# A fused attention and mixture-of-experts kernel: the order of the squares, of the values' norm and of the scales while the weights are prepared

## The chip, the core and the metric

The kernel runs on one core of one Trainium2 chip. The metric is the device time of one execution in microseconds (us), as the median of several runs. Before the change three runs gave 891.67 us in the median, from 890.34 to 894.32.

## What is computed

```python
# attention per batch and head: B=4, H=8, S=576, D=64, M=32
a      = softmax(phi, axis=s)                 # over the 576 positions
k_m    = a^T k ;  v_m = a^T v                 # 32 memory rows each
attn   = softmax(q k_m^T / sqrt(D))           # over the 32 rows
x      = attn v_m                             # (2304, 512) over batches and heads
# gated layer
x      = (sigmoid(x @ w_gate) * (x @ w_val)) @ w_out     # d_ff = 1536
# routed layer, 8 experts, two per token
logits = x @ w_gate + log1p(exp(x @ w_noise)) * noise
top 2 of 8, their softmax as weights
out   += weight * (relu(x @ w1[e]) @ w2[e])              # F = 1024
```

The inputs of the gated layer arrive as 64-bit words, which the kernel reads as pairs of 32-bit words, a low and a high one.

## The kernel before, in words

The program is written in Python generators that are advanced in turns. A scheduler then gives each engine a fixed queue: TensorE (PE), VectorE (DVE), ScalarE (ACT), GpSimd (POOL), and SyncE (SP), which issues nearly all transfers. An engine takes its queue strictly in order, so an instruction that waits holds up all behind it.

The part that the change touches is the first one, the preparation of the gated layer's weights beside the attention of batches 0 and 1.

- **Loads.** 18 blocks of weights (gate and value of six units `u`, then the six blocks of w_out) come as 36 halves of 512 KB through a ring of four buffers (`ws2`, `WB = 4`). `wload_next` asks for one more half after each half is rounded. A load waits until POOL is done with the buffer that it writes to.
- **Rounding** (`rounded`, L325 to L333). Of each half, ACT turns the low words into numbers (L329), DVE puts the high words together in two instructions (L331, L332), and POOL adds both (L333).
- **Norms.** After both halves of a block, ACT squares it with a sum (`AF.Square`, L363 for gate and value, L359 for w_out). `norm2` adds these sums over the partitions by a small matmul (`pmx`, L87), and three or four tiny DVE instructions (L92 to L96) make of that a power of two and its inverse. `values_scale` (L223) does the same with the values' memory rows of a batch, which gives `sv0` for batch 0. `finish` does it for one unit, `w0` to `w5`.
- **Fold** (`fold`, L231). For batch b and unit u, PE multiplies the weights by the values' rows (`pv`, L243). A scale `ws`, made by DVE from unit and batch (L236), goes into `split`: ACT writes the high half-precision part of the product (`wq`, L376), DVE the low part (L377). That is done in four pieces. The tiles `ws` come from a ring of four.
- **Stage 1** (`stage1`, L410). For each third of a batch (a chunk of 192 columns), 24 matmuls (L424) fill two accumulators, ACT takes the tanh with the scale `gs` (L427, made by `gate_scale` at L388 on first use), DVE multiplies (L429), and ACT and DVE write the two parts of `gT` (L430, L431).
- **Stage 2** (`stage2`, L442) multiplies `gT` by the prepared w_out. For that all of w_out has to be rounded, normed and split (`wo`, L376 and L377).

`build` sets the turns. While batch 0's attention runs, and then beside each chunk of batch 0, the generator `weights` is advanced a few steps; each `yield` in it is one step. It has three steps a block here, and three more for each unit's norm. The routed layer follows at about the middle of the span.

## Time and profile before

| | |
|---|---|
| median of the runs | 891.67 us |
| profiled execution | 891.72 us |
| its span, first to last instruction | 889.9 us |
| PE, DVE, ACT, POOL busy | 814.8, 473.5, 456.8, 208.6 us |
| matmuls, DVE, ACT, POOL instructions | 6531, 1317, 907, 210 |
| PE busy, tenths in the first seven slices of 22 us | 5 5 5 8 8 5 9 |

A share of busy time is one of the whole span. In the first 150 us PE is busy for half to nine tenths, and after that almost always, so a stretch's own rows tell more than the sums.

### The profile page before, as it was taken

Reading aid. Unit: us, or ns where it says so; the run is one execution under the profiler, and the core shown is the slowest. Engines: PE = TensorE matmul, PEld = TensorE weight load, DVE = VectorE, ACT = ScalarE, POOL = GpSimd, SP = SyncE. Lnnn points to the kernel's source line nnn. Section 1 sums busy time; section 2 is a strip of 40 time slices with the busy share of each in tenths; the row PEclk is TensorE's granted clock in tenths of the full one; section 3 lists DMA queues with packets and bytes.
Section 4 is the critical chain, followed back from the end, with each engine's and each line's share of the span. In section 5 each row is a group of like instructions: output and inputs, shape, how many; then the busy total and the mean of one; then the engine's idle time right before and its main releaser. Section 6 shows DMA issues by size and latency. Waiting matters only on the chain. (4 is left out here: it accounts for less than half of the span.)

```text
span 889.9 us, 16827 instructions
## 1 busy us (share of the span) xinstructions
PE 814.8 (92%) x6531; PEld 534.0 (60%) x6531; DVE 473.5 (53%) x1317; ACT 456.8 (51%) x907; POOL 208.6 (23%) x210
## 2 busy tenths in 40 slices
PE   5558859999999998898998999999999999999995
PEld 4347746757657765666655656665747556574752
DVE  1788788555647686874443138553444345340110
ACT  3477667615545476672323348564646446461320
POOL 1363440001110201023014443202323122332112
PEclk9998778999999999999999999999999999999998
DMA  9478639324221564546594869826565868473113
GB/s 317 151 258 292 227 115 341 132 75 102 25 78 25 166 214 142 168 166 194 145 346 107 176 132 263 200 95 143 129 188 120 166 141 214 71 117 48 25 13 47
DMA packets 126067, 135.16 MB, mean 152 GB/s; under 512 B 71968, under 2 KB 88480, under 8 KB 125472
## 3 DMA queue, kind: packets, MB, share of 16 engines
q1 hardware_dynamic: 116000, 113.30, 43.9%
q0 software_dynamic: 9984, 20.75, 12.9%
q8 instruction: 52, 0.85, 0.4%
q14 instruction: 31, 0.25, 0.1%
HBM read 87.97 MB, written 30.86 MB: 134 GB/s over the span
## 5 line engine op out<-in xcount | busy, mean ns | idle before, releaser
L424 PE MATMUL pg<-x,wq 128*128 128x192 f16 x1728 | 174.0, 258 | 23.4 <-ACT wq L376 15.1
L424 PEld LDWEIGHTS <-wq 128*128 128x128 f16 x1728 | 152.5, 103 | 44.2 <-ACT wq L376 17.7
L778 PEld LDWEIGHTS <-hT 128*128 128x128 f16 (+1 forms) x960 | 99.8, 105 | 104.8 <-DVE hT L770 0.9
L442 PE MATMUL px<-wo,gT 128*128 128x512 f16 x648 | 148.8, 379 | 0.3 <-issue 0.3
L784 POOL DMA_INDIRECT out<-y,mts x40 | 64.6, 1614 | 208.7 <-ACT y L783 206.9
L778 PE MATMUL py<-w2a,hT 128*128 128x512 f16 (+1 forms) x480 | 105.2, 379 | 0.4 <-DVE hT L770 0.4
L778 PE MATMUL py<-w2b,hT 128*128 128x512 f16 (+1 forms) x480 | 104.9, 379 | 0.0
L764 PE MATMUL ph<-xe,w1a 128*128 128x312 f16 (+2 forms) x768 | 103.3, 296 | 0.0
L770 DVE TENSOR_TENSOR hT<-r,hT 128x312 f16<-128x312 f32 (+2 forms) x128 | 57.4, 480 | 85.9 <-ACT hT L769 84.5
L764 PE MATMUL ph<-xe,w1b 128*128 128x312 f16 (+2 forms) x768 | 103.0, 296 | 0.0
L442 PEld LDWEIGHTS <-gT 128*128 128x128 f16 x648 | 61.5, 98 | 68.6 <-issue 4.5
L783 ACT ACTIVATE y<-py,css 128x512 f32<-128x512 f32 (+1 forms) x40 | 27.5, 687 | 129.6 <-PE py L778 120.6
L764 PEld LDWEIGHTS <-w1b 128*128 128x128 f16 x768 | 75.2, 98 | 27.1
L764 PEld LDWEIGHTS <-w1a 128*128 128x128 f16 x768 | 75.0, 98 | 27.1
L768 ACT ACTIVATE r<-ph 128x312 f32<-128x312 f32 (+2 forms) x128 | 49.7, 428 | 76.5 <-PE ph L764 73.0
L586 POOL DMA_INDIRECT meta<-mt,vi x36 | 36.1, 1003 | 173.8 <-DVE vi L583 46.4
L749 POOL DMA_INDIRECT xg<-xs,mts x40 | 44.4, 1110 | 87.7 <-DMA xe<-xg 49.0
L427 ACT ACTIVATE sg<-pg,gs 128x384 f32<-128x384 f32 x72 | 41.6, 578 | 41.9 <-PE pg L424 27.9
L429 DVE SCALAR_TENSOR_TENSOR pg<-sg,pg 128x384 f32<-128x384 f32 x72 | 40.2, 558 | 36.8 <-PE pg L424 25.7
L781 DVE TENSOR_TENSOR css<-mts,iw 128x1 f32<-128x1 f32 (+1 forms) x40 | 6.5, 164 | 89.5 <-ACT y L783 84.9
L430 ACT ACTIVATE gT<-pg 128x384 f16<-128x384 f32 x72 | 34.8, 485 | 36.7 <-DVE pg L429 34.4
L769 ACT CAST hT<-r 128x312 f16<-128x312 f32 (+2 forms) x128 | 53.1, 458 | 0.8
(311 smaller groups left out, 972.9 us busy)
## 6 DMA issues: line engine op xcount, KB each, us to landing
wo<-w SPq DMA_DIRECT2D x48, 512.0 KB, 5.5
st<-kv SPq DMA_DIRECT2D x16, 512.0 KB, 7.8
f<-w SPq DMA_DIRECT2D x16, 512.0 KB, 3.8
wsp<-hl SPq DMA_DIRECT2D x16, 512.0 KB, 3.5
w<-wg SPq DMA_DIRECT2D x12, 512.0 KB, 5.8
w<-wv SPq DMA_DIRECT2D x12, 512.0 KB, 4.2
w<-wo SPq DMA_DIRECT2D x12, 512.0 KB, 4.2
out<-z SPq DMA_DIRECT2D x23, 256.0 KB, 2.8
```

Of the source, the lines that this page charges most:

```text
L424: nc.tensor.matmul(p[:, f, :], w[:, l, g, j, f * P : (f + 1) * P], x[:, r, g, ch * QC : (ch + 1) * QC], start=n == 0, stop=n == 5)
L427: nc.scalar.activation(sg, ps[0], AF.Tanh, scale=self.gate_scale(b, u))
L429: nc.vector.scalar_tensor_tensor(pv, sg, 1.0, pv, op0=ALU.add, op1=ALU.mult)
L442: nc.tensor.matmul(p, g[:, l, f % 2, t * P : (t + 1) * P], self.wob[f // 2][:, r, f % 2, :], start=f + i == 0, stop=f == FT - 1 and i == 2)
L586: d = nc.gpsimd.indirect_dma_start(out=self.meta, out_offset=bass.IndirectOffsetOnAxis(ap=vi[:, t, k : k + 1], axis=0), in_=mt[:, t, k, :] ...
L749: self.nc.gpsimd.indirect_dma_start(out=xg.rearrange("p a b -> p (a b)"), out_offset=None, in_=self.xs[:rows, :], in_offset=bass.IndirectO ...
L764: nc.tensor.matmul(p[:, : t1 - t0], w1[:, l, k, f * P : (f + 1) * P], xe[:, x, t0:t1], start=n == 0, stop=n == 3 * KT - 1)
L768: nc.scalar.activation(r, p[:, : t1 - t0], AF.Relu, scale=2.0 ** -19)
L769: nc.scalar.copy(self.hT[:, 0, f, t0:t1], r)
L770: nc.vector.tensor_sub(self.hT[:, 1, f, t0:t1], r, self.hT[:, 0, f, t0:t1])
L778: nc.tensor.matmul(py, self.hT[:, l, f, i * P : i * P + m], w2[:, w, f, :], start=n == 0, stop=n == 3 * F2T - 1)
L784: d = nc.gpsimd.indirect_dma_start(out=self.out, out_offset=bass.IndirectOffsetOnAxis(ap=mt[:m, 0:1], axis=0), in_=y[:m], in_offset=None, ...
```

## The change

Three orders are altered.

1. *Squares.* The square of a block is no longer a step of its own after the block's second half. It is issued with the first half of the next block, and tied behind an instruction. `rounded` returns its ACT instruction on the low words (L333 of the new file) as `first`, and the square stands behind that in ACT's queue. The generator now has two steps a block.
2. *Values' norm.* In `norm2`, the first DVE instruction on the values' sum (the one with `floor`) is tied behind the last rounding's second DVE instruction, `self.shifted`.
3. *Scales.* `unit_scales` makes `ws` and `gs` of every pair of batch and unit as soon as both norms are there, in tiles of their own. `fold` and `stage1` only look them up, and `gate_scale` goes.

To make room, the tiles `km` and `ex2` of the attention have one buffer and not two. The ties order instructions of one engine and add no semaphore. The diff, without the lines that only set up the new tables:

```diff
@@ -77,6 +77,9 @@
         nc.vector.tensor_scalar(s, iv, -1, 254 << 23, op0=ALU.mult, op1=ALU.add)
         return s.bitcast(F32), iv.bitcast(F32)
+    def behind(self, d, o):
+        self.tc.add_manual_dep(d.ins, o.ins.name, mybir.DependencyInfo(mybir.DependencyClass.NoSync, mybir.DependencyReason.DATA), reason="order")
+
     def norm2(self, pool, m, tag, before=1, n=1, floor=0):
@@ -86,10 +89,12 @@
         pt = self.pr.tile([P, 512], F32, tag="pr", name="pmx")[:, :n]
         d = nc.tensor.matmul(pt, self.onef, m, start=True, stop=True)
         if self.mark is not None:
-            self.tc.add_manual_dep(d.ins, self.mark.ins.name, mybir.DependencyInfo(mybir.DependencyClass.NoSync, mybir.DependencyReason.DATA), reason="order")
+            self.behind(d, self.mark)
         h, s, iv = (pool.tile([P, n], I32, tag=tag + c, name=tag + c) for c in "hsi")
-        nc.vector.tensor_scalar(h, pt.bitcast(I32), 24, 23, op0=ALU.logical_shift_right, op1=ALU.logical_shift_left)
+        d = nc.vector.tensor_scalar(h, pt.bitcast(I32), 24, 23, op0=ALU.logical_shift_right, op1=ALU.logical_shift_left)
+        if floor and self.shifted is not None:
+            self.behind(d, self.shifted)
         if floor:
             nc.vector.tensor_scalar(h, h, floor << 23, None, op0=ALU.max)
         nc.vector.tensor_scalar(s, h, -1, 204 << 23, op0=ALU.mult, op1=ALU.add)
@@ -188,7 +193,7 @@
-        km = a2.tile([P, 2, 2, D], F32, tag="km", name="km")
+        km = self.a1.tile([P, 2, 2, D], F32, tag="km", name="km")
@@ -227,13 +232,13 @@
         self.nc.scalar.activation(junk, self.flat(self.vbs[b % 2]), AF.Square, accum_out=m)
         self.sv[b], iv = yield from self.norm2(self.cp, m, f"sv{b}", floor=30)
         self.invx.append(iv)
+        self.unit_scales()
     def fold(self, b, u):
         nc = self.nc
         vb = self.vbs[b % 2]
-        s = self.cp.tile([P, 2], F32, tag="ws", bufs=4, name="ws")
-        nc.vector.tensor_scalar(s, self.sw[u], self.sv[b], 2.0 ** -A_BITS, op0=ALU.mult, op1=ALU.mult)
+        s = self.ws[(b, u)]
         t = self.wq[(b, u)] = self.wqp.tile([P, 2, 2, 2, 256], F16, tag="wq", name="wq")
         pv = [self.pg.tile([P, 2, 256], F32, tag="pg", name="pv") for _ in range(2)]
         for j in range(2):
@@ -267,7 +272,7 @@
-            ex = a2.tile([P, n, M], F32, tag="ex" if u < 2 else "ex2", name="ex")
+            ex = (a2 if u < 2 else self.a1).tile([P, n, M], F32, tag="ex" if u < 2 else "ex2", name="ex")
@@ -326,11 +330,12 @@
         nc = self.nc
         lo, hi = t[:, :, 0], t[:, :, 1]
-        nc.scalar.activation(lo, lo.bitcast(U32), AF.Copy, scale=2.0 ** -29)
+        first = nc.scalar.activation(lo, lo.bitcast(U32), AF.Copy, scale=2.0 ** -29)
         w = self.px.tile([P, DM], F32, tag="px", name="pw").bitcast(I32)
         nc.vector.tensor_scalar(w, hi, 3, 0x3FFFFFFF, op0=ALU.logical_shift_left, op1=ALU.bitwise_and)
-        nc.vector.scalar_tensor_tensor(v, hi, -0x40000000, w, op0=ALU.bitwise_and, op1=ALU.bitwise_or)
+        self.shifted = nc.vector.scalar_tensor_tensor(v, hi, -0x40000000, w, op0=ALU.bitwise_and, op1=ALU.bitwise_or)
         nc.gpsimd.tensor_tensor(v, v, lo, op=ALU.add)
+        return first
     def weights(self):
@@ -345,23 +350,33 @@
             self.sw.append(s)
             self.iwg.append(iv[:, 0:1])
             self.iwv.append(iv[:, 1:2])
+            self.unit_scales()
             yield
-        for n, (kind, u) in enumerate(self.wjobs):
-            v = self.flat(self.W[n]) if kind != "wo" else self.flat(self.wob[u + 1]).bitcast(F32)
+        def squares(n, d):
+
+            kind, u = self.wjobs[n]
+            if kind == "wo":
+                q = nc.scalar.activation(junk, vs[n], AF.Square, scale=self.iwv[u], accum_out=self.wom[:, u : u + 1])
+            else:
+                if kind == "wg":
+                    sums[u] = cp.tile([P, 2], F32, tag="wum", bufs=2, name="wum")
+                q = nc.scalar.activation(junk, vs[n], AF.Square, accum_out=sums[u][:, n % 2 : n % 2 + 1])
+            if d is not None:
+                self.behind(q, d)
+
+        vs = [self.flat(self.W[n]) if kind != "wo" else self.flat(self.wob[u + 1]).bitcast(F32) for n, (kind, u) in enumerate(self.wjobs)]
+        for n in range(len(self.wjobs)):
             for h in range(2):
-                self.rounded(self.wts[2 * n + h], v[:, h * 512 : (h + 1) * 512].bitcast(I32))
+                d = self.rounded(self.wts[2 * n + h], vs[n][:, h * 512 : (h + 1) * 512].bitcast(I32))
                 self.wload_next()
+                if h == 0 and n:
+                    squares(n - 1, d)
                 yield
                 if h == 0 and 2 <= n <= 12 and n % 2 == 0:
                     yield from finish(n // 2 - 1, WAIT_W)
-            if kind == "wo":
-                nc.scalar.activation(junk, v, AF.Square, scale=self.iwv[u], accum_out=self.wom[:, u : u + 1])
-            else:
-                if kind == "wg":
-                    sums[u] = cp.tile([P, 2], F32, tag="wum", bufs=2, name="wum")
-                nc.scalar.activation(junk, v, AF.Square, accum_out=sums[u][:, n % 2 : n % 2 + 1])
-            yield
+        squares(n, None)
+        yield
         m = cp.tile([P, 1], F32, name="wom1")
         nc.vector.tensor_reduce(m, self.wom, axis=AX.X, op=ALU.add)
         s, self.cinv = yield from self.norm2(cp, m, "wo")
@@ -382,11 +397,15 @@
         names = "abcd"[:n]
         return t if n == 1 else t.rearrange(f"p {' '.join(names)} -> p ({' '.join(names)})")
-    def gate_scale(self, b, u):
-        if u not in self.gs[b]:
-            g = self.gs[b][u] = self.cp.tile([P, 1], F32, name=f"gs{b}{u}")
-            self.nc.vector.tensor_scalar(g, self.iwg[u], self.invx[b], 0.5, op0=ALU.mult, op1=ALU.mult)
-        return self.gs[b][u]
+    def unit_scales(self):
+        nc = self.nc
+        for b in self.sv:
+            for u in range(len(self.sw)):
+                if (b, u) not in self.ws:
+                    s = self.ws[(b, u)] = self.cp.tile([P, 2], F32, name=f"ws{b}{u}")
+                    nc.vector.tensor_scalar(s, self.sw[u], self.sv[b], 2.0 ** -A_BITS, op0=ALU.mult, op1=ALU.mult)
+                    g = self.gs[(b, u)] = self.cp.tile([P, 1], F32, name=f"gs{b}{u}")
+                    nc.vector.tensor_scalar(g, self.iwg[u], self.invx[b], 0.5, op0=ALU.mult, op1=ALU.mult)
     def batch_scales2(self, b):
         t = self.cp.tile([P, 1], F32, name=f"it{b}")
@@ -424,7 +443,7 @@
                         nc.tensor.matmul(p[:, f, :], w[:, l, g, j, f * P : (f + 1) * P], x[:, r, g, ch * QC : (ch + 1) * QC], start=n == 0, stop=n == 5)
                         n += 1
         sg = self.sp.tile([P, 2, QC], F32, tag="sg", name="sg")
-        nc.scalar.activation(sg, ps[0], AF.Tanh, scale=self.gate_scale(b, u))
+        nc.scalar.activation(sg, ps[0], AF.Tanh, scale=self.gs[(b, u)])
         pv = ps[1]
         nc.vector.scalar_tensor_tensor(pv, sg, 1.0, pv, op0=ALU.add, op1=ALU.mult)
         nc.scalar.activation(o[:, 0, :, cols], pv, AF.Copy, scale=2.0 ** -16)
```

What the queues become is shown at three places. The names w_96 to w_107 are the twelve blocks of gate and value, w_152, w_168 and so on the loaded halves, wo_75 the tile into which the squares' results are thrown away. Line numbers in the rows of the change are those of the new file.

ACT, where batch 0's attention ends (x, L293) and the first blocks are rounded, before:

```order
L293 ACTIVATE x<-pa 128x512
L329 ACTIVATE w_202<-w_202 128x512
L363 ACTIVATE wo_75,wum<-w_96 128x1024
L293 ACTIVATE x<-pa 128x512
L293 ACTIVATE x<-pa 128x2x64
L217 ACTIVATE phi,psm<-phi,pmx 128x576
L329 ACTIVATE w_232<-w_232 128x512
L363 ACTIVATE wo_75,wum<-w_97 128x1024
L217 ACTIVATE phi,psm<-phi,pmx 128x576
```

and now:

```order
L298 ACTIVATE x<-pa 128x512
L333 ACTIVATE w_202<-w_202 128x512
L298 ACTIVATE x<-pa 128x512
L298 ACTIVATE x<-pa 128x2x64
L364 ACTIVATE wo_75,wum<-w_96 128x1024
L364 ACTIVATE wo_75,wum<-w_97 128x1024
L222 ACTIVATE phi,psm<-phi,pmx 128x576
L333 ACTIVATE w_232<-w_232 128x512
L222 ACTIVATE phi,psm<-phi,pmx 128x576
L333 ACTIVATE w_245<-w_245 128x512
L391 ACTIVATE wq<-pv,ws_342 128x256 x2
```

The squares of w_96 and w_97 now stand behind the attention's last copies, and the first scaled weights `wq` follow in the eleventh row. Before, they followed some rows below those shown, behind the square of w_98 too.

DVE, at the scales of unit 5 for batch 0 (w5, sv0), before:

```order
L331 TENSOR_SCALAR pw<-w_1374 128x512
L331 TENSOR_SCALAR pw<-w_1381 128x512
L332 SCALAR_TENSOR_TENSOR wo_81<-w_1374,pw 128x512
L332 SCALAR_TENSOR_TENSOR wo_81<-w_1381,pw 128x512
L236 TENSOR_SCALAR ws<-w5s,sv0s 128x2
L388 TENSOR_SCALAR gs_1547<-w5i,sv0i 128x1
L236 TENSOR_SCALAR ws<-w0s,sv1s 128x2
L236 TENSOR_SCALAR ws<-w1s,sv1s 128x2
```

and now:

```order
L95 TENSOR_SCALAR w5h<-pmx 128x2
L335 TENSOR_SCALAR pw<-w_794 128x512
L100 TENSOR_SCALAR w5s<-w5h 128x2
L101 TENSOR_SCALAR w5i<-w5h 128x2
L336 SCALAR_TENSOR_TENSOR wo_76<-w_794,pw 128x512
L406 TENSOR_SCALAR ws_924<-w5s,sv0s 128x2
L408 TENSOR_SCALAR gs_926<-w5i,sv0i 128x1
```

The scales of unit 5 stood behind the rounding of the last halves of w_out (wo_81); now they stand beside that of the first halves (wo_76).

PE, at the last folds of batch 0, before (w_106 and w_107 are unit 5):

```order
L243 MATMUL pv<-w_106,vb_85 32x256 x8
L243 MATMUL pv<-w_107,vb_85 32x256 x8
L424 LDWEIGHTS wq
L424 MATMUL pg<-x,wq 128x192
L424 LDWEIGHTS wq
L424 MATMUL pg<-x,wq 128x192
```

and now (w_104 and w_105 are unit 4):

```order
L248 MATMUL pv<-w_104,vb_85 32x256 x4
L248 MATMUL pv<-w_105,vb_85 32x256 x2
L248 MATMUL pv<-w_104,vb_85 32x256 x4
L248 MATMUL pv<-w_105,vb_85 32x256 x6
L461 LDWEIGHTS gT
L461 MATMUL px<-wo_75,gT 128x512
L461 LDWEIGHTS gT
L461 MATMUL px<-wo_75,gT 128x512
L443 LDWEIGHTS wq
L443 MATMUL pg<-x,wq 128x192
L443 LDWEIGHTS wq
L443 MATMUL pg<-x,wq 128x192
```

After the fold of unit 4, products of stage 2 (px) now stand between the first matmuls of stage 1. Before, none stood there, nor after the fold of unit 5 until batch 0 was through.

## Rows read from the trace of the kernel before

**Rows 1.** Stretches of the span: busy us of each engine, PE's clock, DMA share, GB/s.

```profile
40.00:160.00 120.00, 88.97 (x993) 69.42 (x993) 100.27 (x238) 86.85 (x180) 45.58 (x56) 0.86 0.74 244
160.00:320.00 160.00, 157.96 (x1648) 109.42 (x1632) 98.74 (x336) 81.05 (x169) 18.05 (x26) 1.00 0.33 87
320.00:480.00 160.00, 145.38 (x1325) 96.53 (x1323) 101.34 (x367) 81.87 (x148) 26.98 (x32) 0.98 0.64 198
480.00:880.00 400.00, 399.58 (x2414) 242.04 (x2412) 154.51 (x321) 190.76 (x375) 107.54 (x79) 1.00 0.58 127
```

**Rows 2.** Timeline of PE: start us, us, what, count, idle before and its end.

```profile
39.62 1.08 PE L243 MATMUL pv<-w,vb 64*32 64x256 f32 x8 [0.17 <-POOL w L333]
40.80 0.59 PE L87 MATMUL pmx<-wum,onef 128*128 128x2 f32 x2
46.49 1.18 PE L424 MATMUL pg<-x,wq 128*128 128x192 f16 x5 [5.10 <-ACT wq L376]
...
84.41 2.15 PE L424 MATMUL pg<-x,wq 128*128 128x192 f16 x24
...
99.78 4.77 PE L424 MATMUL pg<-x,wq 128*128 128x192 f16 x31
...
131.05 0.50 PE L424 MATMUL pg<-x,wq 128*128 128x192 f16 x2 [5.79 <-ACT wq L376]
...
145.55 2.98 PE L442 MATMUL px<-wo,gT 128*128 128x512 f16 x13
```

**Rows 3.** Timeline of ACT.

```profile
33.60 1.06 ACT L363 ACTIVATE wo<-w 128x1024 bf16<-128x1024 f32 x1 [1.00 <-POOL w L333]
...
34.66 0.74 ACT L293 ACTIVATE x<-pa 128x512 f16<-128x512 f32 x2
...
39.60 1.06 ACT L363 ACTIVATE wo<-w 128x1024 bf16<-128x1024 f32 x1 [1.17 <-POOL w L333]
...
45.97 0.82 ACT L376 ACTIVATE wq<-pv,ws 128x256 f16<-128x256 f32 x2
...
130.52 0.84 ACT L376 ACTIVATE wq<-pv,ws 128x256 f16<-128x256 f32 x2 [1.15 <-DVE ws L236]
```

**Rows 4.** Timeline of DVE, first part.

```profile
35.27 0.89 DVE L294 SCALAR_TENSOR_TENSOR x<-pa,x 128x512 f16<-128x512 f32 x2 [0.66 <-ACT x L293]
...
41.43 0.16 DVE L92 TENSOR_SCALAR w0h<-pmx 128x2 int32<-128x2 int32 x1 [1.98 <-PE pmx L87]
...
43.56 0.79 DVE L236 TENSOR_SCALAR ws<-w0s,sv0s 128x2 f32<-128x2 f32 x1
...
82.20 1.28 DVE L331 TENSOR_SCALAR pw<-w 128x512 int32<-128x512 int32 x2
```

**Rows 5.** Timeline of POOL, the roundings of w_97 and of the next half.

```profile
37.02 3.85 POOL L333 TENSOR_TENSOR w<-w,w 128x512 int32<-128x512 int32 x3 [3.45 <-DVE w L332]
```

**Rows 6.** Page, DMA issues: size, median us from issue to landing.

```profile
w<-wg SPq DMA_DIRECT2D x12, 512.0 KB, 5.8
w<-wv SPq DMA_DIRECT2D x12, 512.0 KB, 4.2
```

**Rows 7.** Waits of SP's queue from 30 to 130 us: sum, times, longest.

```profile
SPq L318 <- POOL w L333: 37.0, 20, 7.2
```

**Rows 8.** Timeline of DVE at the scales of unit 5 and after.

```profile
128.31 1.27 DVE L332 SCALAR_TENSOR_TENSOR wo<-w,pw 128x512 int32<-128x512 int32 x2
129.50 0.93 DVE L236 TENSOR_SCALAR ws<-w5s,sv0s 128x2 f32<-128x2 f32 x1
...
131.58 0.22 DVE L236 TENSOR_SCALAR ws<-w1s,sv1s 128x2 f32<-128x2 f32 x1
...
142.18 1.28 DVE L377 SCALAR_TENSOR_TENSOR wo<-wo,wos,wo 128x1024 f16<-128x1024 f32 x1
```

**Rows 9.** Timeline of SP, the zeros written to the output.

```profile
133.25 16.96 SPq L512 DMA_DIRECT2D out<-z  x23
```

**Rows 10.** A stretch with a low clock, columns as in Rows 1.

```profile
99.00:105.00 6.00, 5.60 (x38) 5.11 (x37) 5.05 (x9) 2.71 (x6) 2.48 (x2) 0.58 0.40 132
```

More of the change, by code (lines that the diff above doesn't have):

```diff
@@ L294, in turned @@
             nc.vector.scalar_tensor_tensor(ol, src, 2.0 ** A_BITS, oh, op0=ALU.mult, op1=ALU.subtract)
-        self.gs[b] = {}
         ex = {}
@@ L903, in build @@
         self.gs, self.it, self.gT, self.pxs, self.lg, self.itx, self.mt = {}, {}, {}, {}, {}, {}, {}
-        self.snapped, self.sv, self.sw, self.wq = False, {}, [], {}
+        self.snapped, self.sv, self.sw, self.wq, self.ws = False, {}, [], {}, {}
         m1, mw, mraw, wsc = self.m1, _, _, _ = ExitStack(), ExitStack(), ExitStack(), ExitStack()
@@ L924, in build @@
         self.whalves = [(k, u, h) for k, u in self.wjobs for h in range(2)]
-        self.wts, self.mark, self.wanted = [], None, []
+        self.wts, self.mark, self.shifted, self.wanted = [], None, None, []
         self.att_first_loads(0)
```

## The prediction

> **What bounds the kernel now.** I read the stretches of the span first. From 160 us on PE is busy nearly all the time, for 158.0 of 160 us, then 145.4 of 160, then 399.6 of 400. From 40 to 160 us it is busy for only 89.0 of 120, at a mean granted clock of 0.86 [rows 1]. So what the change is worth is decided before 160 us, and a microsecond that PE starts its later work sooner is kept as long as the 14.6 us without work between 320 and 480 do not grow. In the stretch to 160 us the fullest engine is DVE with 100.3 us, then PE, then ACT with 86.9 [rows 1]. All this DVE work has to be done in either order before batch 1 is under way, so the stretch can shrink only by DVE's 120 − 100.3 = 19.7 us without work, or by PE doing in its gaps what it now does later.
>
> The timelines show where the gaps come from. At the front PE ends the fold of unit 0 at 40.7 us and waits until 46.49 us for the scaled weights, 5.10 us of it with nothing in its queue able to run [rows 2]. The chain behind that: the attention's copies on ACT stand behind a square and begin at 34.66 us [rows 3]; DVE waits 0.66 us for them, and the rounding of w_97 comes behind [rows 4]; POOL gets it at 37.02 us, and its first two additions end two thirds into 3.85 us, at 39.6 us [rows 5]; there the square of w_97 begins [rows 3], the sum over the partitions follows at 40.80 us [rows 2], the norm at 41.43 us and the scale at 43.56 us, with roundings between [rows 4]; ACT writes the first `wq` at 45.97 us [rows 3]. At the back PE waits 5.79 us before unit 5's stage 1 [rows 2]. ACT had been waiting there for the scale `ws` of unit 5 and goes on at 130.52 us [rows 3], and DVE made that scale at 129.50 us, straight behind the last roundings of w_out [rows 8].
>
> **The change, part by part.** All of it is set against the profiled execution, 891.72 us, which lies 0.05 us from the median of the runs.
>
> *The front: squares and values' norm.* The square of 1.06 us no longer holds the copies at 34.66 us [rows 3], which is worth up to 1.06 us. Of DVE's two instructions a half, which follow each other at about 0.6 us (two take 1.28) [rows 4], the first for w_97 and the second for w_96 no longer fall behind the last copies, about 1.1 us more. The norm of unit 0 thus comes some 2.2 us sooner. From the norm to `wq` it took 45.97 − 41.43 = 4.5 us [rows 3, 4], with three halves' instructions and a square between; now little but the scales stands there. `wq` may come another 2.4 us sooner, but that rounding is only moved behind it. I take −2.2 us; the ends are −1.1 (the square alone) and −4.6.
>
> *The roundings come forward.* With two steps a block and not three, `weights` runs ahead: the last rounding of w_out, which stood before unit 5, now stands beside unit 3. DVE's work is the same, but each half must be loaded into one of four buffers first. One turn of that ring is a landing of 4.2 to 5.8 us [rows 6], 1.2 us on DVE [rows 4], 1.28 us on POOL [rows 5], and some 0.5 us until SP issues the next. SP's queue already waits 37.0 us in 20 waits for POOL to free a buffer [rows 7]. With a landing of 4.5 us (nearer to the lower row, since fewer transfers of keys and values now fall between) a turn is 7.5 us, 1.9 us a half, against 1.2 us of DVE. Some 15 halves lie between the norm of unit 0 and the end of unit 1's `wq`, so 15 × 0.7 = 10.5 us of possible waiting. To fill it DVE has eight pieces of `wq` at about 0.4, three chunks at about 0.95 and some 2 us of norms, 8.0 us. I take +2.5 us. The ends are 0 and, if every landing is 5.8 us over the 7.5 turns left, another 7.5 × 1.3 = 9.8 us on top. Units 1 to 3 come later than before, by up to the roundings that now precede them; that alone costs nothing, as those roundings are then missing in front of units 4 and 5.
>
> *The scales.* The 5.79 us wait before unit 5 [rows 2] goes, since its `ws` is made long before. What is late next is w_out's split. Its six pieces of 1.28 us on DVE [rows 8] now stand around units 4 and 5, and two of them (2.56 us) fall ahead of unit 5's `wq`, which itself needs 0.82 us for two pieces on ACT [rows 3] and about 0.4 us on DVE. I take 5.79 − 2.56 − 1.22 = −2.0 us, between 0 and −5.8. The number of `ws` and `gs` instructions stays the same. Two of the `ws` took 0.79 and 0.93 us where another took 0.22 [rows 4, 8]; if the ring of four tiles is why, the separate tiles give back 1.3 us. I take 0.
>
> *Stage 2 in the gaps.* By the fold of unit 4 for batch 1, PE's queue now holds 30 products of stage 2 where it held 19. Those 11, at 2.98 / 13 = 0.23 us [rows 2], fill gaps and need not be done later: −2.5 us, between 0 and −2.5.
>
> *Other moves.* The single buffers of `km` and `ex2` make a copy wait for its reader, some 0.4 us a batch by the copies' row [rows 3], beside other work; I take 0, with +0.8 as the other end. In SP's queue two loads of batch 2's keys and values now stand behind nine of the 23 zero writes, which take 16.96 us together [rows 9]: 6.6 us later, and still well before batch 2 needs them, so 0; without that cover PE would wait for part of the 6.6.
>
> **Sum:** −2.2 + 2.5 − 2.0 − 2.5 = −4.2 us, thus 891.7 − 4.2 = **887.5 us**. About 0.5%, here 4.5 us, is what a measurement can tell from no change, so the forecast lies at that edge.
>
> **The clock.** In the rows, 24 matmuls of stage 1 take 2.15 us (0.090 each), and 31 others take 4.77 us (0.154 each) [rows 2], in a stretch where the granted clock is 0.58, after waits [rows 10]. A chunk at the lower level thus costs 24 × 0.064 = 1.5 us more. [...]
>
> **The rivals.**
>
> 1. *The ring becomes the bound; slower.* All 30 halves after unit 0 land in 5.8 us. For it speaks the row of the gate blocks [rows 6] and SP's long waits [rows 7]; against it the value blocks' 4.2 us. −4.2 + 9.8 = +5.6, 897.3 us. It decides for a loss above 0.5% from a landing of about 4.5 + (4.2 + 4.5) / 7.5 = 5.7 us on. [...]
> 2. *The wait only moves; no change.* The scales of unit 5 are early, but `wq` waits for the split of w_out as long as it did for `ws`. The front and the ring cancel and only the products of stage 2 stay: about −2.2, 889.5 us. For it: DVE is the fullest engine [rows 1], and all its work stays.
> [...]
> 4. *More is gained.* With the roundings through early, half of DVE's 19.7 us goes: −9.9, 881.8 us. For it: the waits in the last third, 5.79 us being the largest, all have a rounding in front of them.
>
> **How the numbers follow.** The forecast has 0.40, of which I count 0.23 beyond 4.5 us and 0.17 within; rival 1 has 0.15, rival 2 0.22, rival 3 0.05, rival 4 0.18. That makes faster 0.23 + 0.18 = 0.41, same 0.17 + 0.22 = 0.39, slower 0.15 + 0.05 = 0.20. The likeliest case alone reaches from about 884 to 890. The range reaches to the rivals' ends and a little beyond the fourth, as the front may give its 4.6 us and the scales all of their 5.8: 878.5 to 897.5 us.
>
> **What would show it.** The front holds if the first `wq` starts between 41 and 44 us and not at 46. The ring holds if the last rounding of w_out is done between 100 and 112 us and DVE waits for loads between 47 and 70 us. The scales hold if PE's wait before unit 5 is under 4 us, with a split of w_out ahead of it. Stage 2 holds if its first products run before unit 4's stage 1 ends. The forecast is wrong if DVE's time without work from 40 to 160 us falls by more than 8 us or grows, or if PE's stretches after 160 us take on new waits.

## The result: slower by 0.8%

The changed kernel takes 897.85 us in the median of 20 runs (892.47 to 901.43), the kernel before 890.60 us in 20 runs beside it (883.04 to 897.26). The ratio is 1.0081, with a 95% interval of 1.0058 to 1.0103: 7.25 us slower, beyond the 0.5% that the forecast took for what a measurement can tell. The forecast was 887.5 us, and 897.85 lies just above the range's upper end of 897.5. Profiled, the changed kernel has a span of 898.3 us (before 889.9). The rows below are of one execution each, of 900.04 us for the change and of 891.72 us before.

The stretches of the changed kernel, with the columns of [rows 1]:

```profile
40.00:160.00 120.00, 81.19 (x844) 62.20 (x844) 91.54 (x224) 80.38 (x162) 44.86 (x56) 0.77 0.77 245
160.00:320.00 160.00, 157.96 (x1711) 110.28 (x1705) 99.47 (x337) 84.29 (x180) 18.09 (x26) 1.00 0.30 81
320.00:480.00 160.00, 147.07 (x1352) 97.80 (x1353) 103.39 (x352) 84.68 (x147) 24.25 (x31) 0.97 0.65 198
480.00:880.00 400.00, 397.46 (x2420) 241.42 (x2418) 158.99 (x353) 193.83 (x384) 106.10 (x79) 1.00 0.58 129
```

Against [rows 1], the loss arises before 160 us. PE does 81.2 us of work there and not 89.0. DVE, of which the forecast said that it can only lose idle time, gains some: 120 − 91.5 = 28.5 us without work, before 19.7. From 160 us on PE is as full as before, so what is late at 160 us stays late. The tanh instructions on ACT, one for each chunk and unit, say how late: at the fourth unit (unit 3) 22.7 us, at the first of batch 1 11.4 and at the 25th of the 72 (200 us) 7.35. The routed layer's first product (`ph`, at 470.55 us) is still 7.5 us late.

ACT at the front and at unit 3's first tanh:

```profile
41.65 0.85 ACT L391 ACTIVATE wq<-pv,ws 128x256 f16<-128x256 f32 x2
...
50.44 0.68 ACT L333 ACTIVATE w<-w 128x512 int32<-128x512 uint32 x1 [1.98 <-DMA w<-wv]
51.00 1.06 ACT L364 ACTIVATE wo<-w 128x1024 bf16<-128x1024 f32 x1
...
52.59 0.48 ACT L391 ACTIVATE wq<-pv,ws 128x256 f16<-128x256 f32 x1
...
53.90 0.57 ACT L446 ACTIVATE sg<-pg,gs 128x384 f32<-128x384 f32 x1
...
118.65 0.56 ACT L446 ACTIVATE sg<-pg,gs 128x384 f32<-128x384 f32 x1
```

The first `wq` starts 4.3 us sooner than in [rows 3]. But the last piece of unit 0's `wq` starts at 52.59 us, behind low words that waited 1.98 us for a load, and a square. Before, it ran at 49.81. So the first tanh is 3.4 us later (before 50.49). The front's gain is gone within one unit. The same three places on ACT before, the last the first tanh of unit 3:

```profile
49.81 0.47 ACT L376 ACTIVATE wq<-pv,ws 128x256 f16<-128x256 f32 x1
50.49 0.58 ACT L427 ACTIVATE sg<-pg,gs 128x384 f32<-128x384 f32 x1 [0.22 <-PE pg L424]
...
95.94 0.58 ACT L427 ACTIVATE sg<-pg,gs 128x384 f32<-128x384 f32 x1
```

PE at units 0, 1 and 3, and at the end of batch 0:

```profile
52.43 3.54 PE L443 MATMUL pg<-x,wq 128*128 128x192 f16 x21 [4.14 <-DVE wq L392]
...
70.44 0.48 PE L443 MATMUL pg<-x,wq 128*128 128x192 f16 x2 [4.02 <-DVE gT L450]
73.82 0.59 PE L90 MATMUL pmx<-wum,onef 128*128 128x2 f32 x2 [2.90 <-ACT wo L364]
...
113.72 0.66 PE L443 MATMUL pg<-x,wq 128*128 128x192 f16 x3 [6.77 <-DVE wq L392]
...
134.09 0.59 PE L461 MATMUL px<-wo,gT 128*128 128x512 f16 x2 [0.93 <-ACT wo L391]
```

DVE at that wait of 6.77 us:

```profile
107.58 0.69 DVE L335 TENSOR_SCALAR pw<-w 128x512 int32<-128x512 int32 x1 [0.20 <-DMA w<-wo]
110.92 0.69 DVE L335 TENSOR_SCALAR pw<-w 128x512 int32<-128x512 int32 x1 [2.65 <-DMA w<-wo]
111.53 0.55 DVE L450 SCALAR_TENSOR_TENSOR gT<-pg,gT 128x384 f16<-128x384 f32 x1
111.99 1.27 DVE L336 SCALAR_TENSOR_TENSOR wo<-w,pw 128x512 int32<-128x512 int32 x2
113.19 0.48 DVE L392 SCALAR_TENSOR_TENSOR wq<-pv,ws,wq 128x256 f16<-128x256 f32 x1
```

Unit 3's fold was done on PE, and its `wq` needed 0.48 us of DVE. It stood behind roundings of w_out, which nothing needs before stage 2, and one of these stood there for 2.65 us until its half had landed. PE's waits from 40 to 160 us (sum, times, longest) say the same in sum:

```profile
PE pg L443 <- DVE wq L392: 16.7, 6, 6.8
PE pmx L90 <- ACT wo L364: 7.5, 4, 2.9
PE pg L443 <- ACT wq L391: 4.9, 5, 2.8
PE pg L443 <- DVE gT L450: 4.0, 1, 4.0
```

and before:

```profile
PE pg L424 <- ACT wq L376: 15.1, 7, 5.8
PE pmx L87 <- ACT wo L363: 5.4, 3, 4.1
PE pg L424 <- DVE wq L377: 3.7, 7, 0.9
```

The 5.79 us before unit 5 [rows 2] are gone; no wait of PE between 131 and 152 us is longer than 0.93. The last rounding of w_out is added up by POOL at 116.18 us, before at 130.36.

### The profile page after: what moved, and what is told of

Its sections match the earlier page's. It is cut to its first block, busy times and chain, and to the rows that moved or that the text cites. A ratio compares the mean times of both kernels' runs of the same rounds, so it can differ in the third digit from the quotient of the medians.

```text
span 898.3 us, 16813 instructions
## 1 busy us (share of the span) xinstructions
PE 815.8 (91%) x6531; PEld 533.0 (59%) x6531; DVE 471.7 (53%) x1317; ACT 460.6 (51%) x909; POOL 206.2 (23%) x210
## 5 line engine op out<-in xcount | busy, mean ns | idle before, releaser
L443 PEld LDWEIGHTS <-wq 128*128 128x128 f16 x1728 | 150.7, 102 | 54.2 <-DVE wq L392 19.0
L461 PE MATMUL px<-wo,gT 128*128 128x512 f16 x648 | 151.9, 383 | 1.2 <-ACT wo L391 0.9
```

What stands on the lines that cost most here:

```text
L443: nc.tensor.matmul(p[:, f, :], w[:, l, g, j, f * P : (f + 1) * P], x[:, r, g, ch * QC : (ch + 1) * QC], start=n == 0, stop=n == 5)
L461: nc.tensor.matmul(p, g[:, l, f % 2, t * P : (t + 1) * P], self.wob[f // 2][:, r, f % 2, :], start=f + i == 0, stop=f == FT - 1 and i == 2)
```

## The experiments

**The theories.** Theory A is the pace. A unit took nine steps of `weights` before: two blocks of three and three of the norm. Its callers take nine a unit as well, three behind each of three chunks. With two steps a block a unit takes seven, and `weights` runs ahead by two steps a unit. Counted in DVE's order, 7, 21, 26, 35 and 36 halves (of 36) now stand ahead of the first `wq` of units 0 to 4, where there were 8, 17, 21, 26 and 30. Theory B is the squares' new place behind the next low words, B' their tie there, C the scales, D the values' norm, E an optimum of the pace near that of before. The kernel before took 885.7 to 892.0 us in the five comparisons, so the verdicts go by ratios to the kernel before of the same comparison. A run is called slower or faster where its interval doesn't hold 1; of 19 such intervals about one is to be expected to miss by chance. All of them together:

| run | halves ahead of units 1 to 4 | unit 3's first tanh, us | ratio, 95% interval |
|---|---|---|---|
| before | 17, 21, 26, 30 | 95.94 | 1 |
| the change | 21, 26, 35, 36 | 118.65 | 1.0081 [1.0058, 1.0103] |
| e2_before_fast | 21, 25, 35, 36 | 119.14 | 1.0038 [1.0005, 1.0071] |
| h1_after_half | 21, 27, 35, 36 | 119.53 | 1.0067 [1.0043, 1.0092] |
| t1_notie | 21, 25, 34, 36 | 115.00 | 1.0031 [1.0011, 1.0052] |
| e5_fast | 21, 25, 34, 36 | 115.51 | 1.0025 [0.9997, 1.0053] |
| f1_all_foldfirst | 16, 22, 30, 36 | 105.47 | 1.0045 [1.0021, 1.0069] |
| e1_pace | 17, 21, 26, 29 | 102.62 | 1.0048 [1.0019, 1.0077] |
| q1_all_pace_notie | 17, 21, 26, 30 | 95.94 | 1.0077 [1.0048, 1.0105] |
| h3_e1_half | 17, 23, 28, 30 | 97.71 | 1.0022 [0.9996, 1.0047] |
| e7_sqpace | 17, 22, 27, 31 | 101.91 | 1.0011 [0.9982, 1.0040] |
| e9_norm | 17, 21, 26, 30 | 95.62 | 1.0007 [0.9977, 1.0036] |
| e5_norm_scales | 16, 21, 26, 30 | 93.92 | 1.0008 [0.9985, 1.0031] |
| e6_scales | 16, 21, 26, 29 | 100.44 | 0.9988 [0.9960, 1.0016] |
| h2_before_half | 17, 23, 28, 31 | 95.43 | 0.9999 [0.9974, 1.0025] |
| p2_all_turns22 | 16, 21, 26, 28 | 98.70 | 0.9986 [0.9961, 1.0011] |
| q3_turns22_notie | 16, 20, 25, 28 | 98.40 | 0.9997 [0.9970, 1.0024] |
| p3_all_turns12 | 13, 18, 23, 26 | 93.88 | 1.0005 [0.9975, 1.0035] |
| p1_scales_pre2 | 13, 18, 22, 25 | 91.77 | 1.0014 [0.9992, 1.0035] |
| f2_scales_foldfirst | 14, 20, 25, 26 | 89.32 | 0.9981 [0.9956, 1.0006] |

The first tanh is read in one profiled execution of each kernel. That of e1_pace (899.23 us, median 895.1) is the second slowest of its twelve. Those of q1 (885.00 us, median 892.2), h2, p1, p3 and f2 are the fastest of theirs, so q1's trace doesn't show the loss that its ratio has.

**The old pace under the three orders (e1_pace), and the new pace under none of them (e2_before_fast).**

```diff
 e1_pace, from the change
                     yield from finish(n // 2 - 1, WAIT_W)
+            yield
         squares(n, None)
 e2_before_fast, from before
                 nc.scalar.activation(junk, v, AF.Square, accum_out=sums[u][:, n % 2 : n % 2 + 1])
-            yield
+        yield
```

> All three orders of the change, with one more step at the end of each block of the weights' preparation, so that a block takes three steps again as before. Theory A, the pace: with two steps a block the roundings of later units stand in DVE's, ACT's and PE's queues ahead of the pieces that units 1 to 3 wait for, and that is the whole loss. Then this kernel is no slower than the one before (886 to 891 us, ratio 0.995 to 1.000), unit 3's fold starts near 90 us and not at 103, PE's waits for DVE's wq from 40 to 160 us fall from 16.7 to under 8 us, and PE is busy there for 88 us or more. Theory B, the orders: the square tied behind the next block's low words makes the sums and norms late. Then it stays at 895 to 899 us (ratio 1.005 to 1.009), with waits of pmx for the square as in the change (7.5 us in 4).

> The kernel before, with the step behind each square left out: two steps a block, and no other part of the change. Theory A, the pace: 895 to 899 us (ratio 1.005 to 1.009), unit 3's fold starts at 98 us or later (before 89.7), and DVE's time without work from 40 to 160 us grows from 19.7 to 26 us or more. Theory B, the orders: 889 to 892 us (ratio 0.998 to 1.002), as none of the three orders is in it.

The pace alone makes the kernel before slower, by 0.38%, and its trace has the change's picture: unit 3's first tanh at 119.14 us, DVE busy for 93.9 us of 120, and PE waiting 9.8 us for DVE's `wq`, 6.1 of them at once. Stretch 40 to 160 us, then PE's first two waits in it:

```profile
40.00:160.00 120.00, 87.65 (x917) 65.29 (x914) 93.89 (x227) 82.75 (x170) 45.02 (x56) 0.77 0.75 242
```

```profile
PE pg L424 <- DVE wq L377: 9.8, 4, 6.1
PE pg L424 <- ACT wq L376: 8.0, 6, 3.8
```

So Theory A holds for a part, but 0.38% is not 0.81%, and its interval is only just clear of 1. And e1_pace, forecast at 0.995 to 1.000 by A, kept 0.48%, below B's 1.005 by a hair. The marks of both are in its trace: PE waits only 3.7 us for DVE's `wq`, as A had it, and 6.6 us in 4 for the square, as B had it. In its trace a square is late in the way B says: behind low words that wait for a load stand `gT`, the square and `wq` of unit 1:

```profile
67.96 0.67 ACT L333 ACTIVATE w<-w 128x512 int32<-128x512 uint32 x1 [2.05 <-DMA w<-wg]
68.52 0.48 ACT L450 ACTIVATE gT<-pg 128x384 f16<-128x384 f32 x1
68.89 1.06 ACT L364 ACTIVATE wo<-w 128x1024 bf16<-128x1024 f32 x1
69.83 0.20 ACT L364 ACTIVATION_READ_ACCUMULATOR wo<-w 128x1 f32 x1
70.61 0.87 ACT L392 ACTIVATE wq<-pv,ws 128x256 f16<-128x256 f32 x2 [0.57 <-DVE wq L393]
```

**One order at a time, at three steps a block (e6_scales, e7_sqpace, e9_norm), and two of them (e5_norm_scales).**

```diff
 e6_scales: of the change, unit_scales and the tiles in a1 alone
+            self.unit_scales()
 e7_sqpace, from before: squares(n - 1, d) with its tie alone, the third step kept
+                if h == 0 and n:
+                    squares(n - 1, d)
...
             yield
+        squares(n, None)
+        yield
 e9_norm, from before: the tie in norm2 alone; e5_norm_scales: e6 and e9
+        if floor and self.shifted is not None:
+            self.tc.add_manual_dep(d.ins, self.shifted.ins.name, ..., reason="order")
```

> The kernel before with the scales alone, made as soon as the norms are known; squares, values' norm and three steps a block as before. Theory A, the pace: 887 to 891 us (ratio 0.996 to 1.000); PE's wait of 5.8 us before unit 5 falls under 4 us, which is worth at most 2 us. Theory C, the scales: 24 small instructions of DVE stand at the norms, ahead of the pieces that the unit then waits for, and cost 0.2 us each in front of units 0 to 3, so 893 to 895 us (ratio 1.003 to 1.005).

> The kernel before with the squares alone, each tied behind the next block's first low words, at three steps a block; scales and values' norm as before. Theory A, the pace: 887 to 891 us (ratio 0.996 to 1.000); the attention's copies no longer wait for a square of 1.06 us, and unit 0's first wq may start 1 to 2 us sooner than at 46 us. Theory B, the orders: each unit's sum waits for the next half's landing, so that pmx stands in PE's queue for some 2 us at units 1 to 4: 895 to 899 us (ratio 1.005 to 1.009).

> The kernel before with the values' norm alone: its first instruction on DVE tied behind the second instruction of a rounding; squares, scales and three steps a block as before. Theory D, the norm: the tie delays the scale of the values and so unit 0's first wq, and every later unit with it: 893 to 895 us (ratio 1.003 to 1.005), which would be the part of the 4.2 us (all three orders at the old pace) that the squares alone (+1.0) and the scales alone (-1.1) don't show. Rival, the interaction: each order alone is within 2 us of before, and only together, in one queue, do they cost: 889 to 892 us (ratio 0.998 to 1.002).

> Norm and scales together, squares and three steps a block as before. Theory B, the squares: the loss of 4.2 us at the old pace comes in with the squares alone, since ACT then waits for a half's landing ahead of the square on which the next unit's norm rests; so this kernel is at 888 to 891 us (ratio 0.997 to 1.000). Theory D, the norm: 893 to 895 us (ratio 1.003 to 1.005).

None of the three can be told from no change: −0.12%, +0.11%, +0.07%. C falls, and so does B for the squares alone. D's lower end, 1.003, is still inside the intervals of e9_norm and e5_norm_scales, at their upper edge. The norm and the scales together are at +0.08%, so most of the 0.81% comes in with the change's first part, the squares and the step dropped with them. In e5_norm_scales the first tanh runs at 46.28 us, 4.2 us sooner than before; the end is no sooner.

**Half the loads (h1_after_half, h2_before_half).** Each half loads 256 KB instead of 512. Every loaded column is used twice, so these kernels compute other numbers.

```diff
-            src, k = a[:, u * 256 : (u + 1) * 256].rearrange(...)[:, 2 * h : 2 * h + 2], 2
+            src, k = a[:, u * 256 : (u + 1) * 256].rearrange(...)[:, 2 * h : 2 * h + 1], 1
...
-        lo, hi = t[:, :, 0], t[:, :, 1]
+        lo, hi = two(t[:, 256:, :].rearrange("p f t -> p (f t)")), twice(t[:, :256, 1])
```

> The changed kernel with half of each weight half loaded (256 KB for 512 KB; each loaded column is used twice, so the numbers computed are others). All instructions on DVE, ACT and POOL keep their sizes. Theory A with the loads as its cause: units 1 to 3 wait because the roundings ahead of them in the queues wait for landings, at 2.7 us a half from the 8th to the 28th in both kernels. With half the bytes the changed kernel is then within 2 us of the kernel before with the same half loads, and below 888 us. Rival, the engines' own time: the roundings ahead cost by their busy time on DVE (1.2 us a half), whatever the loads take; then the changed kernel stays 6 us or more above the other.

> The kernel before with half of each weight half loaded, in the same way; the other half of the pair. Theory A with the loads: DVE's waits for landings (2.3 us from 40 to 130 us) and ACT's (5.1 us) go, the last rounding of w_out ends before 115 us and not at 131, and the time is 880 to 888 us. Rival, the engines' own time: 888 to 891 us, as the engines' queues stay as long.

The rival is the nearer one. With half the bytes the change still loses 0.67%, and the kernel before gains nothing (0.9999). By these ratios the two are 6 us apart, as the rival had it. By the medians, 896.86 and 892.20 us, they are 4.7 apart, which lies between the theories. Nor did the last addition of h2_before_half come before 115 us: it starts at 128.0. Stretch 40 to 160 us of h1_after_half, then DVE's waits in it:

```profile
40.00:160.00 120.00, 81.29 (x860) 62.30 (x861) 94.64 (x232) 81.03 (x166) 45.15 (x56) 0.90 0.54 170
```

```profile
DVE pg L452 <- PE pg L447: 6.0, 7, 1.8
...
DVE pw L339 <- DMA w<-wo: 1.1, 1, 1.1
DVE wo L396 <- ACT wo L395: 0.9, 2, 0.5
DVE pw L339 <- DMA w<-wg: 0.8, 1, 0.8
```

and the waits for loads in the change:

```profile
DVE pw L335 <- DMA w<-wo: 3.6, 3, 2.6
DVE pw L335 <- DMA w<-wg: 2.1, 3, 0.8
DVE pw L335 <- DMA w<-wv: 1.7, 2, 1.1
```

DVE's waits for loads fall from 7.4 us in the change to 1.9, and the DMA share from 0.77 to 0.54. PE's work in the stretch is the same, 81.3 us against 81.2, and unit 3 is as late. The pace of the roundings is also the same: on ACT the 9th and the 29th half start 48.3 us apart (in the change 49.1). One reservation: with shorter loads the scheduler put 15 halves ahead of unit 0, where the change has 7, so the two orders aren't alike at the front; from unit 1 on the counts are.

**Fewer steps by the callers (p2_all_turns22, p3_all_turns12, p1_scales_pre2), and the tie (t1_notie).**

```diff
 p2_all_turns22, from the change (p3: 1 for 4; p1: e6_scales with 2 for 4 alone)
-            turns(*[weights] * (4 if self.sv else 1), atts)
+            turns(*[weights] * (2 if self.sv else 1), atts)
...
-                turns(weights, weights, weights)
+                turns(weights, weights)
 t1_notie, from the change
-            if d is not None:
-                self.behind(q, d)
```

> The changed kernel, all three orders and two steps a block, but with fewer steps of the weights' preparation taken by its callers: two for four ahead of unit 0, two for three behind each chunk. On DVE 8, 16, 21, 26 and 28 halves now stand ahead of the first wq of units 0 to 4, where the change has 7, 21, 26, 35 and 36 and the kernel before 8, 17, 21, 26 and 30. Theory A, the pace (each half ahead of a wq holds the unit up, by some 2.7 us a half): 890 to 895 us (ratio 0.999 to 1.004), like the three orders at three steps a block (+4.2) or better, unit 3's fold at 89 to 95 us. Rival, the change's own code holds the loss: 896 to 899 us.

> As the run before, with one step for four ahead of unit 0 and two for three behind each chunk: 7, 13, 18, 23 and 26 halves ahead of the first wq of units 0 to 4, fewer than in the kernel before. Theory A, the pace: the units come sooner than before, unit 3's fold at 80 to 87 us, and the time is 884 to 890 us (ratio 0.993 to 0.999). Rival E, the pace has an optimum near that of before: w_out is rounded, normed and split later, stage 2 of batch 0 starts later and PE waits behind 141 us instead: 891 to 896 us.

> The scales alone, at three steps a block, with two for four steps ahead of unit 0: 7, 13, 18, 22 and 25 halves ahead of the first wq of units 0 to 4. Theory A, the pace: 882 to 888 us (ratio 0.990 to 0.997), the fastest kernel here. Rival E, an optimum near before: 889 to 893 us, with a later last rounding of w_out (over 135 us) and waits of PE for w_out's split behind 141 us.

> The changed kernel without the tie of the square to the next block's first low words; the pace stays (7, 21, 25, 34 and 36 halves ahead of the first wq). Theory B', the tie costs 3 to 4 us of the 7 (the three orders at the old pace stood 3.6 us above norm and scales alone): 893 to 895 us (ratio 1.003 to 1.005). Rival, the tie costs nothing by itself (squares alone stood at +1.0, not to be told from nothing): 896 to 899 us (ratio 1.006 to 1.010).

p2_all_turns22 is the plainest run of the study: all three orders, tie included, and only the callers take fewer steps. It loses nothing (0.9986). Its stretch 40 to 160 us:

```profile
40.00:160.00 120.00, 90.35 (x1014) 70.49 (x1015) 97.39 (x235) 87.60 (x180) 46.17 (x57) 0.82 0.70 220
```

PE does 9.2 us more there than in the change. Fewer steps still gain nothing, as E said: p3 and p1 bring unit 3 some 2 and 4 us sooner than before and end at 1.0005 and 1.0014. E's reason isn't in p1's trace, though: PE's waits from 140 to 200 us sum to 1.4 us there, before to 2.2. So why it gains nothing stays open. The change without the tie stands at 1.0031, where B' had put it.

**What was left (q1_all_pace_notie, h3_e1_half, f1_all_foldfirst, f2_scales_foldfirst, e5_fast, q3_turns22_notie).** q1 is e1_pace, and q3 p2_all_turns22, without the tie. h3 is e1_pace with half loads. e5_fast is e5_norm_scales with e2's edit. f1 and f2 put each fold of batch 0 ahead in the scheduler, in the change and in e6_scales:

```diff
-            self.fold(0, u)
+            with ahead_by(100):
+                self.fold(0, u)
```

> The three orders at three steps a block, without the tie of the square to the next block's low words. Theory B', the tie costs at this pace too: back to 889 to 892 us against 890.6 of before (ratio 0.998 to 1.002). Rival: the 4.2 us there are not the tie's, but come from where the scheduler put other work, and it stays at 1.003 to 1.006.

> The three orders at three steps a block, tie kept, with half of each weight half loaded (each loaded column is used twice, so the numbers computed are others). If the tie costs because ACT waits for a half's landing ahead of the square (2.05 us ahead of unit 1's gT, square and wq in the trace with full loads), then the ratio falls to that of the kernel before with half loads (0.9999), within 0.998 to 1.002. Rival: the landing is not the cause, ratio 1.003 to 1.006.

> The changed kernel with each fold of batch 0 given a scheduling priority of 100 ahead, so that a unit's wq stands in DVE's and ACT's queues ahead of more roundings: 7, 16, 22, 30 and 36 halves ahead of units 0 to 4, at the change's pace of two steps. Theory A, the place in the queue: units 1 and 2 come as early as before (the first wq behind 16 and 22 halves, not 21 and 26), unit 3's first tanh at about 106 us (35 halves: 118.7; 26 halves: 95.9), and the time is 1.001 to 1.005 of before. Rival, the number of steps costs in itself: 1.006 to 1.010.

> The scales alone at three steps a block, with the same priority for the folds: 7, 14, 20, 25 and 26 halves ahead of units 0 to 4, against 8, 17, 21, 26 and 30 before. Theory A: units 1 to 4 come 2 to 8 us sooner than before, and the time is 0.993 to 0.998. Rival E, an optimum near before: 0.999 to 1.003, since w_out is then rounded and split later.

> Norm and scales, squares in their old place, and two steps a block: the change without its squares' move, at its pace (7, 21, 25, 34 and 36 halves ahead of units 0 to 4). At three steps a block this stood at 1.0008. Theory A, the pace: 1.003 to 1.008, as the pace alone on the kernel before (1.0038) and the change without the tie (1.0031). Rival, the move of the squares holds the whole loss: 0.999 to 1.002.

> All three orders with fewer steps by the callers, without the tie: 8, 16, 20, 25 and 28 halves ahead. With the tie it stood at 0.9986. Theory A, the pace alone decides: 0.996 to 1.001 again. Rival, the new place of the square costs by itself (as the three orders at three steps a block without the tie, 1.0077, would say): 1.004 to 1.009.

The tie falls as a cause of its own: without it the change is better (1.0081 to 1.0031, intervals that don't overlap), e1_pace not (1.0048 to 1.0077), p2_all_turns22 neither (0.9986 to 0.9997). h3 lies between its theories, and so does e5_fast, whose interval holds 1. f1 gives back less than half, within A's range. f2, the version nearest to beating the kernel before, is at 0.9981 with an interval that holds 1: none of the runs beats it beyond what can be told.

**What the runs show together.** Five kernels have 34 or 35 halves ahead of unit 3. In all of them its first tanh runs at 115 to 119.5 us, whatever else they hold, and their ratios are 1.0025 to 1.0081. Of thirteen with 22 to 28 halves there, eleven start at 89 to 102 us and stand at 0.9981 to 1.0022; the other two are e1_pace and q1_all_pace_notie. The callers' steps alone take the whole loss out of the changed kernel. f1, with 30, lies between in both. So it is shown that the units' start follows the number of halves ahead of their `wq`. It is also shown that the pace costs time, by two pairs that differ in nothing else: e2 against the kernel before, and the change against p2. With a lead of 34 or more the cost is 0.25 to 0.38% without the squares' tie (e2, t1, and e5_fast, which can't be told from nothing), 0.67 and 0.81% with it (h1 and the change). What the tie adds at this pace is one pair of runs (1.0081 and 1.0031), and at a smaller lead it adds nothing.

Not explained are e1_pace and q1_all_pace_notie: 26 halves, and 1.0048 and 1.0077. Their counts are like those of p2 and q3 only up to unit 4. Ahead of unit 5 they have 36 and 35 halves, where p2 and q3 have 32 and 31, and their first tanh of unit 5 runs at 142.4 and 137.5 us, that of p2 and q3 at 130.0 and 127.9. But the kernel before has 36 there too (134.7 us), so that alone doesn't explain it. In e1_pace the lag behind the kernel before grows to 8.4 us at unit 4 and is still 8.2 at 200 us, and the low words of the 9th and of the 29th half start 54.3 us apart, before 49.8. What slows them stays open; the 2.05 us above are one place, and halving the loads there didn't decide it. The granted clock, taken up at the end of the next section, is a rival for these two as well.

## Why the prediction was wrong, point by point

- **The front** held for its own mark: the first `wq` starts at 41.65 us, within 41 to 44. It was worth nothing, because the next pieces of the same `wq` stood behind roundings (52.59 us against 49.81).
- **The step that failed** is in the part on the roundings: "Units 1 to 3 come later than before, by up to the roundings that now precede them; that alone costs nothing, as those roundings are then missing in front of units 4 and 5." Measured, unit 3 came 22.7 us later, and the roundings missing later gave back 15.4 of them by 200 us, not all. The likely reason is in the forecast's own first paragraph: DVE is the fullest engine before 160 us (100.3 us of 120), and PE is full after (158.0 of 160). While PE waited for `wq`, DVE waited in turn for loads, for PE's sums and for ACT (28.5 us idle, 7.4 of them put down to loads, 3.4 to the sums, 8.2 to ACT), and of what both lose before 160 us the part that is left at 200 us (7.35 us) comes back nowhere. e2_before_fast measures the pace alone at +0.38%, 3.4 us; in the changed kernel, against p2_all_turns22, it is 0.95% or 8.5 us.
- **The term of the ring**, +2.5 us, assumed 1.9 us a half once the halves come forward. Its 0.5 us until SP issues the next load, an estimate without a row, is 0.4 in the trace of before: POOL ends an addition at 46.36 us, and SP's issue starts at 46.39 and takes 0.37. On ACT the low words of the 9th and of the 29th half start 49.1 us apart in the change (45.56 and 94.69) and 49.8 before (46.69 and 96.48): 2.5 us a half in both. The halves came forward in the order of the instructions, but over these 20 hardly in time: the 21st came 8.3 us sooner, and at the 29th 1.8 were left. Only the last six came sooner for good, by 2 to 13 us, and the last addition runs at 116.18 us, past the 100 to 112 of the forecast. Its other mark came: from 47 to 70 us DVE waited 3.1 us for loads, before 0.9.
- **Rival 1**, the ring as the bound, gave 897.3 us, nearly the time measured, but by long landings, and these are not the cause: with half the bytes to land the loss stays (h1_after_half). What the rival had right is that the units wait for the roundings put ahead of them. That a load waits until POOL has freed a buffer is in the change as before (from 30 to 130 us SP waits 39.0 us in 21 for `w`, before 37.0 in 20), and a larger ring was not tried.
- **The scales** held in kind: the 5.79 us before unit 5 are gone. Alone they measure −0.12% (−1.1 us, not to be told from nothing) against −2.0. The ring of four tiles wasn't why some `ws` took long: with tiles of their own two still took 0.62 and 0.92 us.
- **Stage 2 in the gaps** held: 29 of its products run before 160 us in the rows, before 19, and the lag falls from 9.7 us at batch 1's fold of unit 4 to 7.35. What the products gain by themselves no run shows: p2 has 9 of them before 160 us and loses nothing, e2 has 32 and loses 0.38%.
- **The clock.** Units 4 and 5, which rival 3 (0.05) had at the low clock, ran at a higher granted clock than before, 1.00 for 0.77. Their two stretches, the change first:

```profile
130.00:158.00 28.00, 26.25 (x299) 18.60 (x299) 23.20 (x55) 18.03 (x34) 1.45 (x2) 1.00 0.75 246
...
112.00:142.00 30.00, 20.56 (x219) 17.01 (x219) 25.64 (x72) 19.38 (x42) 10.44 (x28) 0.77 0.56 164
```

  For the units ahead of them the clock stays a rival, and there the column can't be taken as it stands. From 42 to 52 us it shows 1.00 for the kernel before and 0.50 for the change, and yet stage 1's matmuls took 358 and 359 ns in the mean. From 54 to 60 us, at 1.00 again, they took 246 ns in the kernel before. The rows, two of the kernel before, two of the change, and the last of the kernel before from 54 us on:

```profile
42.00:52.00 10.00, 4.27 (x22) 2.82 (x23) 8.74 (x23) 7.28 (x14) 5.87 (x5) 1.00 0.81 259
L424 PE MATMUL pg<-x,wq 128*128 128x192 f16 x20 | 4.1, 358 | 5.8 <-ACT wq L376 5.1 <-ACT sg L427 0.3 <-DVE wq L377 0.3
...
42.00:52.00 10.00, 3.25 (x15) 1.78 (x15) 7.65 (x20) 6.76 (x13) 6.35 (x5) 0.50 0.88 294
L443 PE MATMUL pg<-x,wq 128*128 128x192 f16 x13 | 2.8, 359 | 5.6 <-ACT wq L391 3.4 <-DVE wq L392 2.2
...
L424 PE MATMUL pg<-x,wq 128*128 128x192 f16 x38 | 3.5, 246 | 1.1 <-ACT sg L427 1.1
```

  So from 42 to 52 us the kernel before ran its matmuls as slowly as the change did at 0.50. Counting the front of a trace at 0.50 as long as its matmuls take that time (in the kernel before until about 53 us) gives, as an estimate, a mean clock from 40 to 160 us of 0.80 before, not the 0.86 of [rows 1], and of 0.77 in the change (for h1_after_half 0.78, not the 0.90 above). It is 0.76 to 0.78 in the change, e2, h1, e5_fast, f1, e1 and q1, which stand at 1.0025 to 1.0081. It is 0.79 to 0.86 in t1_notie (0.80, at 1.0031) and in the eleven at 0.9981 to 1.0022. So it goes with the loss about as the halves do, and in e1 and q1 where they don't. No run holds the clock and changes the waits, so whether the lower clock is a part of the cause or only follows PE's waits stays open.

  In the change's trace the column is at 1.00 from 34 to 39.4 us and at 0.50 from 40 to 60 us; PE's wait of 2.78 us for the first `wq` begins at 39.41. No run shows whether the wait brings the lower clock.
- **The mark for being wrong**, DVE's idle time growing, is the one that came: 28.5 us for 19.7.

## What to carry to other kernels

Where a generator's steps are interleaved with other work, taking a step out of it is a change of its own: count the steps of a unit against the turns that its callers take, and count on the bound engine how many instructions then stand ahead of the work that others wait for. Work that is moved ahead in program order need not be done sooner (here 2.5 us a half in both kernels, and what sets that pace no run shows); it makes others wait behind it (unit 3 here by 22.7 us), and not all of that need come back (here 15.4 us by 200 us). A change of several orders is tested one by one and with the pace held. A clock column that shows 1.00 at the front of a trace is checked against the matmuls' own times (here 358 ns at 1.00 and 359 ns at 0.50).

## What had not been expected of the hardware

Halving the bytes of 36 loads of 512 KB changed nothing in the time (0.9999), although the DMA engines were busy for 0.74 of the stretch from 40 to 160 us and DVE and ACT had waits for these loads in the trace (2.3 and 5.1 us from 40 to 130 us). The share fell to 0.52, and ACT still waited for loads (6.7 us from 40 to 130 us). SP still waited 37.2 us in 21 for POOL to free a buffer of `w` from 30 to 130 us, before 37.0 in 20. So here a wait that the trace put down to a load was no sign that a shorter load would help.
